# A third kind of expert step, for up to 64 rows, in a block-attention and top-1 expert kernel

## The chip, the core and the metric

The kernel runs on one core of a Trainium2 chip. The metric is device time in microseconds (us) of one execution. Of the core's engines, PE (TensorE) multiplies matrices and its weight loads are listed apart as PEld, DVE (VectorE) and ACT (ScalarE) do elementwise work, POOL (GpSimd) issues the transfers that gather and scatter by index, and SP (SyncE) issues the other transfers. All of SP's transfers go through one queue.

## What is computed

Block-causal attention over 8 batches, 8 heads, 576 positions, head size 64; its output, seen as 4608 rows of 512 numbers, goes through a layer of eight experts of which each row uses one:

```python
e_idx = np.argmax(x @ w_gate, axis=1)
...
for e in range(E):
    mask = e_idx == e
    h = np.maximum(x[mask] @ w1[e], 0.0)      # 512 -> 1024
    ye = h @ w2[e]                            # 1024 -> 512
    out[mask] = gate_w[mask, None] * eom[mask, e, None] * ye
```

All numbers are float32. The kernel splits each float32 operand into a float16 part ("hi") and a bfloat16 rest ("lo"), and multiplies hi by hi, hi by lo and lo by hi, so every product of two tiles is three matmuls. With the inputs drawn, the experts get 896, 0, 1030, 58, 512, 192, 384 and 1536 rows.

## The kernel before

The first half of the span is attention; its matmuls are woven with the flips (transpositions) of the softmax and with the routing. The last stage runs the experts in **steps**. A step takes rows of one expert, in tiles of 128 rows: kind P (pair) two tiles, up to 256 rows; kind S (single) one tile, up to 128 rows. `ORDER` (line 53) lists the kinds in the order in which steps run, `NKIND` how many steps of a kind may ever be needed. The routing (`route_rest`, line 639) counts on the chip how many steps of each kind each expert needs, and writes three small tables, one entry per step: the first row (`rti`), the expert (`wsel`) and whether the weights have to be loaded (`wneed`). Steps that the list `ORDER` can't hold run in a second block behind an `If` on `more`; with these rows the 17 P and 4 S of `ORDER` are just what is needed.

A step i is made of:

- `fetch_ids`, `fetch_x` (POOL): the rows' numbers, then the rows themselves, gathered from `x_d` into `xg`, three and more steps ahead;
- `turn_x`: ACT casts `xg` to `xr` (hi), DVE subtracts (lo), SP transposes both into `xt` by a DMA, two steps ahead;
- `fetch_w` (SP): w1 and w2 of the expert, 2 MB each, in four quarters each, into `w1f` and `w2f`, of which there is one each. An expert that the step before had already is not loaded again (the four issues stand in the queue, but their condition is false); a step of kind S, and a P behind an S, always loads;
- `split_w1`, `split_w2`: ACT casts each quarter to `w1b`/`w2b` (line 777), DVE subtracts (line 778); eight of each per step, loaded anew or not. `w1b` and `w2b` are double, and steps alternate;
- `stage_h` (line 889 PE, 897 ACT, 898 DVE): h = relu(x w1), transposed: 96 matmuls with a 128x128 block of w1 as the stationary operand and the rows as the moving one (256 columns for P, 128 for S), in two halves of 48; after each half ACT takes the relu into `hh` and DVE the rest into `hl`;
- `stage_y` (line 916): per tile of 128 rows 24 matmuls with 128x128 blocks of `hh` or `hl` stationary and w2 moving, 512 columns; ACT scales the result into `ys` (line 919), POOL scatters it to `out` (line 920).

`run` (line 1033) sets the order of the expert stage. In turn i PE does h(i), then y(i-1). ACT and DVE do: relu of the first half of h(i), `turn_x` of step i+2, the split of w1 for step i+1, relu of the second half, the scaling of y(i-1), the split of w2 for step i+1. SP issues w1 and w2 of step i+1 (each quarter when the split before has freed its buffer), then the transposition of step i+2. An engine runs its list strictly in this order.

Of the kernel before, what the change touches and what calls it, by code (L numbers as in the profile page):

```python
# [20 lines left out]
P = 128  # L21
# [5 lines left out]
def block_attention_top1_moe(  # L27
# [22 lines left out]
    SCALE = D ** -0.5  # L50


    ORDER = "PPPPPSPPPPSPPPPSPPPPS"
    KINDS = "PS"
    NKIND = (22, 8)
    FKIND = tuple(ORDER.count(kind) for kind in KINDS)
    BKIND = (0, NKIND[0])
    NSTEP = sum(NKIND)
    NPAIR = NKIND[0]
    NXG = 3  # L60
# [554 lines left out]
        nc.vector.tensor_scalar(row0, t64[:, 0:8:2], fe, None, ALU.add)  # L615


    def sequence(order, i0, used):
        seq = []
        for i, kind in enumerate(order):  # L620
            k = KINDS.index(kind)
            seq.append((BKIND[k] + used[k], 2 - k, i0 + i))
            used[k] += 1
        return seq

    used = [0, 0]
# [12 lines left out]
    def route_rest():  # L639

        cnt = counts(B, "cnt1")
        room, used = sb.tile([P, 2 * NK[4]], F32, name="pt4"), [0]

        def scratch(shape):
            n = 1
            for x in shape:
                n *= x
            used[0] += n
            r = room[:, used[0] - n:used[0]]
            return r.rearrange("p (a b) -> p a b", b=shape[1]) if len(shape) == 2 else r  # L650


        nc.vector.scalar_tensor_tensor(cnt, first, 7 * 64.0 + 1, cnt, ALU.mult, ALU.max)
        big = scratch([E, NTE])
        nc.vector.tensor_tensor(big, bc(cnt, [P, E, NTE], 2), bc(t64, [P, E, NTE], 1), ALU.is_gt)
        nk = small.tile([P, 2, E], F32, name="nk", bufs=1)
        nc.vector.tensor_reduce(nk[:, 0], big[:, :, 2:NTE:4], AX.X, ALU.add)
        nc.vector.tensor_reduce(nk[:, 1], big[:, :, 0:NTE:4], AX.X, ALU.add)
        nc.vector.tensor_tensor(nk[:, 1], nk[:, 1], nk[:, 0], ALU.subtract)

        room3 = sb.tile([P, 2 * NK[3]], F32, name="pt3")[:, 0:3 * E * E].rearrange("p (k a b) -> p k a b", k=3, a=E)
        c1, cm = room3[:, 0], room3[:, 1:3]
        nc.vector.tensor_tensor(c1, upto, bc(first, [P, E, E], 1), ALU.max)
        nc.vector.tensor_tensor(cm, bc(c1, [P, 2, E, E], 1), bc(nk, [P, 2, E, E], 2), ALU.mult)
        cum = small.tile([P, 2, E], F32, name="cum", bufs=1)
        nc.vector.tensor_reduce(cum, cm, AX.X, ALU.add)

        own = small.tile([P, 2, E], F32, name="own", bufs=1)
        nc.vector.tensor_tensor(own, nk, cum, ALU.subtract)
        nc.vector.tensor_tensor(own, own, bc(first, [P, 2, E], 1), ALU.mult)  # L670
        nc.vector.tensor_tensor(cum, cum, own, ALU.add)
        beg = small.tile([P, 2, E], F32, name="beg", bufs=1)
        nc.vector.tensor_tensor(beg, cum, nk, ALU.subtract)
        tot = small.tile([P, 2], F32, name="tot", bufs=1)
        nc.vector.tensor_reduce(tot, cum, AX.X, ALU.max)

        mo = small.tile([P, 1], F32, name="mo", bufs=1)
        nc.vector.tensor_scalar(mo, tot[:, 0:1], float(FKIND[1] - FKIND[0]), tot[:, 1:2], ALU.add, ALU.max)
        nc.vector.tensor_copy(more, mo)

        sh = [P, NSTEP, E]
        inn = scratch(sh[1:])
        ge = scratch(sh[1:])
        parts = [(slice(b, b + n), n) for b, n in zip(BKIND, NKIND)]
        for kind, (sl, n) in enumerate(parts):
            idx = bc(tcol[:, 0:n], [P, n, E], 2)
            nc.vector.tensor_tensor(inn[:, sl], idx, bc(beg[:, kind], [P, n, E], 1), ALU.is_ge)
            nc.vector.tensor_tensor(ge[:, sl], idx, bc(cum[:, kind], [P, n, E], 1), ALU.is_ge)
        nc.vector.tensor_tensor(inn, inn, ge, ALU.subtract)

        nc.vector.tensor_tensor(ge, inn, bc(ecol, sh, 1), ALU.mult)
        et = small.tile([P, NSTEP], F32, name="et", bufs=1)
        nc.vector.tensor_reduce(et, ge, AX.X, ALU.add)
        nc.vector.tensor_copy(wsel, et)
        diff = small.tile([P, NSTEP], F32, name="diff", bufs=1)
        nc.vector.tensor_tensor(diff[:, 1:], et[:, 1:], et[:, 0:NSTEP - 1], ALU.not_equal)
        nc.vector.memset(diff[:, NPAIR:], 1.0)
        for c in fresh:
# [7 lines left out]
        nc.vector.scalar_tensor_tensor(base[:, 1], nk[:, 0], 2.0 * P, e0, ALU.mult, ALU.add)  # L706
        for kind, (sl, n) in enumerate(parts):
# [37 lines left out]
    def fetch_x(st, halves=None):  # L745
        c, n, i = st
        for h in range(*(halves or (0, n))):
            nx = NTOK - 2 * S if 2 * i + h < 3 else NTOK
            nc.gpsimd.indirect_dma_start(
                out=xg[i % NXG][:, h], out_offset=None, in_=x_d[0:nx, :],  # L750
                in_offset=IOA(ap=ids[i][:, h, 0:1].bitcast(U32), axis=0), bounds_check=nx - 1, oob_is_err=False,
            )

    def rows_of(w, ev, j):
# [150 lines left out]
    def stage_y(st, halves=None):  # L905
# [2 lines left out]
        hh, hl = hs[i]  # L908
        w2h, w2l = w2b[b][:, 0], w2b[b][:, 1].bitcast(BF16)
        prods = ((hh, w2h), (hh, w2l), (hl, w2h))  # L910
        for h in range(*(halves or (0, n))):
            py = ps_t.tile([P, 512], F32, name="ps_t")
            k = 0
            for f in range(KF):
                for hv, wv in prods:
                    nc.tensor.matmul(py, hv[:, f, h], wv[:, f, :], start=(k == 0), stop=(k == 3 * KF - 1))  # L916
                    k += 1
            ys = fs.tile([P, DM], F32, name="ys", bufs=4)
            act = nc.scalar.activation(ys, py, AF.Copy, scale=ids[i][:, h, 1:2].bitcast(F32))  # L919
            nc.gpsimd.indirect_dma_start(  # L920
                out=out, out_offset=IOA(ap=ids[i][:, h, 0:1].bitcast(U32), axis=0), in_=ys, in_offset=None,
                bounds_check=NTOK - 1, oob_is_err=False,
            )
# [191 lines left out]
```

## Time and profile before

| | |
|---|---|
| median of three runs (all) | 823.86 us (822.45, 823.86, 830.36) |
| the profiled execution | 826.82 us |
| its span, first to last instruction | 825.1 us |
| PE busy | 764.0 us (93%) |
| DVE, ACT busy | 547.1, 517.5 us |
| clock granted to TensorE, mean | 0.982 of full speed |

A row of the timeline gives a start in us from the beginning of the span, a duration, the engine, the line of the code, the tiles and shapes, and how often the instruction comes in a row; in square brackets the idle time of the engine ahead of it and what ended it. The start of one matmul to the start of the next is what a matmul costs in a stream; its own duration is longer, since they overlap.

### The profile page before, as it was taken

The numbers are of one execution on the slowest core, as the hardware profiler recorded it, in microseconds if no ns is written. First come the engines' busy times: TensorE is split into PE (matmuls) and PEld (weight loads), VectorE is DVE, ScalarE is ACT, GpSimd is POOL, SyncE is SP. The second block draws the span as 40 slices with busy tenths as digits, with TensorE's granted clock in tenths as the row PEclk, the third lists the DMA queues.
The fourth block names the chain that finished last, engine by engine and source line by source line (L and its number), as shares of the span: only waits on it lengthen the run. The fifth ranks groups of instructions, "written<-read, shape, count | busy, mean of one in ns | idle before, by whom it ended". The sixth has DMA issues, their size and how long they took to land. (4 is left out here: it accounts for less than half of the span.)

```text
span 825.1 us, 17693 instructions
## 1 busy us (share of the span) xinstructions
PE 764.0 (93%) x6466; PEld 512.7 (62%) x6466; DVE 547.1 (66%) x1200; ACT 517.5 (63%) x1207; POOL 252.6 (31%) x219
## 2 busy tenths in 40 slices
PE   4899988898989889778999999999999999999994
PEld 3566656565656656555686666676657666676652
DVE  5787858677676767858572866786566656786530
ACT  5788776777758667567513855765556555775530
POOL 4322312424122242447245432233212333200001
PEclk9999999999999999889999999999999999999998
DMA  8998997989898797996029899793789958721601
GB/s 153 168 185 174 192 176 148 176 150 184 173 205 151 155 183 157 191 226 177 28 83 270 152 369 257 220 275 99 249 264 280 274 188 281 179 50 48 230 27 41
DMA packets 255887, 148.25 MB, mean 180 GB/s; under 512 B 224561, under 2 KB 224625, under 8 KB 255793
## 3 DMA queue, kind: packets, MB, share of 16 engines
q1 hardware_dynamic: 247520, 127.76, 69.4%
q0 software_dynamic: 8272, 19.29, 7.6%
q8 instruction: 53, 0.87, 0.5%
q14 instruction: 42, 0.34, 0.1%
HBM read 122.23 MB, written 19.73 MB: 172 GB/s over the span
## 5 line engine op out<-in xcount | busy, mean ns | idle before, releaser
L889 PEld LDWEIGHTS <-w1b 128*128 128x128 f16 (+1 forms) x2112 | 182.6, 98 | 25.2 <-ACT ys L919 2.0
L355 ACT ACTIVATE pt<-ps_s,nbs 128x448 f32<-128x448 f32 (+1 forms) x314 | 164.4, 535 | 41.8 <-DVE nbs L343 17.9
L889 PE MATMUL ps_s<-xt,w1b 128*128 128x256 f16 (+3 forms) x1824 | 182.1, 261 | 1.8 <-DMA xt<-xr 1.5
L916 PE MATMUL ps_t<-w2b,hh 128*128 128x512 f16 x608 | 181.0, 379 | 0.0
L778 DVE TENSOR_TENSOR w2b<-w2f,w2b 128x1024 bf16<-128x1024 f32 x76 | 88.0, 1219 | 113.4 <-ACT w2b L777 113.4
L423 PE MATMUL ps_t<-ident,pt 128*128 128x128 f32 x800 | 124.5, 283 | 8.2 <-DVE xn L472 3.9
L429 ACT COPY pT<-ps_t 128x512 f32<-128x512 f32 (+3 forms) x222 | 96.5, 463 | 56.4 <-PE ps_t L423 55.6
L97 POOL TENSOR_TENSOR sp<-nat,sp 128x1152 f16<-128x1152 f32 x30 | 71.2, 2374 | 152.8 <-DVE nbs L343 91.7
L916 PE MATMUL ps_t<-w2b,hl 128*128 128x512 f16 x304 | 115.2, 379 | 0.0
L919 ACT ACTIVATE ys<-ps_t,ids 128x512 f32<-128x512 f32 x38 | 26.1, 687 | 136.1 <-PE ps_t L916 112.1
L335 PE MATMUL ps_s<-tr,tr 128*128 128x448 f16 (+1 forms) x378 | 98.8, 284 | 11.4 <-ACT pt L355 10.9
L920 POOL DMA_INDIRECT out_dram<-ys,ids x38 | 44.9, 1181 | 185.0 <-ACT ys L919 130.2
L916 PEld LDWEIGHTS <-hh 128*128 128x128 f16 x608 | 59.3, 98 | 66.8 <-issue 0.2
L423 PEld LDWEIGHTS ps_t<-ident,pt 128*128 128x128 f32 x800 | 87.3, 143 | 15.6 <-DVE xn L472 4.2
L336 PE MATMUL ps_s<-sw,tr 128*128 128x448 f16 (+1 forms) x378 | 91.4, 283 | 1.8 <-DMA sw<-tr 1.3
L438 PE MATMUL ps_a<-pT,va 128*64 128x512 f32 (+3 forms) x256 | 85.5, 457 | 6.8 <-DMA va<-in_v_dram 5.7
L778 DVE TENSOR_TENSOR w1b<-w1f,w1b 128x1024 bf16<-128x1024 f32 x76 | 88.1, 1218 | 0.5 <-ACT w1b L777 0.2
L393 DVE TENSOR_REDUCE nmx<-ps_s 128x2 f32<-128x896 f32 (+1 forms) x63 | 60.2, 955 | 41.7 <-PE ps_s L338 41.1
L438 PE MATMUL ps_a<-pT,vb 128*64 128x512 f32 (+3 forms) x256 | 85.6, 458 | 2.0 <-DMA vb<-in_v_dram 2.0
L777 ACT CAST w1b<-w1f 128x1024 f16<-128x1024 f32 x76 | 74.1, 1045 | 1.2 <-DMA w1f<-in_moe_w_dram 1.2
L777 ACT CAST w2b<-w2f 128x1024 f16<-128x1024 f32 x76 | 73.6, 1042 | 0.0
L355 ACT ACTIVATION_READ_ACCUMULATOR pt<-ps_s,nbs 128x1 f32 x314 | 65.2, 208 | 0.0
(203 smaller groups left out, 1080.2 us busy)
## 6 DMA issues: line engine op xcount, KB each, us to landing
w1f<-in_moe_w_dram SPq DMA_DIRECT2D x76, 512.0 KB
w2f<-in_moe_w_dram SPq DMA_DIRECT2D x76, 512.0 KB
nat<-in_k_dram SPq DMA_DIRECT2D x15, 576.0 KB
nat<-in_q_dram SPq DMA_DIRECT2D x15, 576.0 KB
sw<-tr SPq DMA_DIRECT2D x30, 288.0 KB
x_d<-xn SPq DMA_DIRECT2D x32, 256.0 KB
va<-in_v_dram SPq DMA_DIRECT2D x32, 128.0 KB
vb<-in_v_dram SPq DMA_DIRECT2D x64, 64.0 KB
```

What stands on the lines that cost most here:

```text
L97: last_lo[0] = lo.tensor_tensor(sp[:, :, 1, :], self.nats[i], sp[:, :, 0, :], ALU.subtract)
L335: nc.tensor.matmul(ps_ap, qq, k1[ab][:, c0:c1], start=True, stop=False)
L336: nc.tensor.matmul(ps_ap, qq, k2[ab][:, c0:c1], start=False, stop=last)
L355: last_exp[0] = nc.scalar.activation(to, ap, AF.Exp, bias=nbs[0:r, t, ab:ab + 1], scale=SCALE, accum_out=sums[0:r, t, hA + ab:hA + ab + 1],)
L393: nc.vector.tensor_reduce(nmx[:, t, :], pX[:, :, 0:n], AX.X, ALU.max, negate=True)
L423: nc.tensor.transpose(ps[:, i], probs[t][:, col:col + P], ident)
L429: copies[next(nth)](pT[:, r:r + m, Q0[t]:Q0[t] + rows], ps[:, i:i + m, 0:rows])
L438: nc.tensor.matmul(pa[64 * a:64 * a + 64, P * j:512], (va, vb)[a][:, j, :], pT[:, 1 + 2 * j + a, 64 + P * j:576], start=(j == 0), stop=False,)
L777: nc.scalar.copy(hi, src)
L778: eng.tensor_tensor(lo, src, hi, ALU.subtract)
L889: nc.tensor.matmul(ph[:, f4].rearrange("p (h n) -> p h n", n=P), wv[:, cc, f, :], xv[:, cc], start=(k == 0), stop=(k == 3 * KD - 1))
L916: nc.tensor.matmul(py, hv[:, f, h], wv[:, f, :], start=(k == 0), stop=(k == 3 * KF - 1))
```

## The change

A third kind of step, H, takes up to 64 rows. `ORDER` becomes 16 P, 3 S and 3 H, 22 steps where there were 21; the routing counts three kinds. Rows of an expert beyond its full pairs go to an H (1 to 64 rows), an S (65 to 128), an S and an H (129 to 192) or a further P (193 and more). With the rows above:

| | steps in order (kind and expert; * marks those whose weights are loaded) |
|---|---|
| before | P2 P2 P2* P2 P0* S2* P0* P0 P4* P4 S0* P5* P6* P7* P7 S3* P7* P7 P7 P7 S6* |
| after | P2 P2 P2* P2 H2* P0* P0 S0* P0* P4* H3* P4* P6* S5* P7* P7 H5* P7* P7 P7 P7 S6* |

(The first two steps load ahead of the table. Steps count from 0, so H stands at 4, 10 and 16.) H, like S, always loads, and so does a P behind it.

In an H step h has 64 moving columns instead of 128. The second layer is turned (`turned_y`): 96 matmuls with 128x128 blocks of w2 stationary and `hh`/`hl` moving, 64 columns, so the result stands transposed in PSUM; ACT copies it to SBUF, and four transpositions on PE turn it back. These and the scaling and scattering are owed (`owed`, `pay`) until the first quarter of the first half of the next h has been issued. An H step gathers and scatters 64 rows instead of 128.

```diff
-    ORDER = "PPPPPSPPPPSPPPPSPPPPS"
-    KINDS = "PS"
-    NKIND = (22, 8)
+    ORDER = "PPPPHPPSPPHPPSPPHPPPPS"
+    KINDS = "PSH"
+    KTILES = (2, 1, 1)
+    KROWS = (2 * P, P, 64)
+    NKIND = (19, 8, 8)
...
-        nk = small.tile([P, 2, E], F32, name="nk", bufs=1)
-        nc.vector.tensor_reduce(nk[:, 0], big[:, :, 2:NTE:4], AX.X, ALU.add)
-        nc.vector.tensor_reduce(nk[:, 1], big[:, :, 0:NTE:4], AX.X, ALU.add)
-        nc.vector.tensor_tensor(nk[:, 1], nk[:, 1], nk[:, 0], ALU.subtract)
...
+        nc.vector.tensor_reduce(over, big.rearrange("p e (n j) -> p j e n", j=4), AX.X, ALU.add)
+        nk = small.tile([P, NKD, E], F32, name="nk", bufs=1)
+        nc.vector.tensor_copy(nk[:, 0], over[:, 3])
+        nc.vector.tensor_tensor(nk[:, 1], over[:, 1], over[:, 3], ALU.subtract)
+        nc.vector.tensor_tensor(nk[:, 2], over[:, 0], over[:, 2], ALU.add)
+        nc.vector.tensor_tensor(nk[:, 2], nk[:, 2], over[:, 1], ALU.subtract)
+        nc.vector.tensor_tensor(nk[:, 2], nk[:, 2], over[:, 3], ALU.subtract)
...
     def stage_h(*args, **kw):
         for act in h_steps(*args, **kw):
-            pass
+            pay()
         return act
+
+    def pay():
+        while owed:
+            owed.pop()()
...
-        m = h1 - h0
-        xh, xl = (x[:, :, h0:h1] for x in xs[i])
+        m, w = h1 - h0, width[i]
+        xh, xl = (x[:, :, h0:h1, 0:w] for x in xs[i])
...
+        if width[i] < P:
+            return turned_y(st, prods)
...
+    def turned_y(st, prods):
+
+        i = st[2]
+        w = width[i]
+        pt = ps_a.tile([P, 512], F32, name="ps_a")[:, 0:KD * w].rearrange("p (c n) -> p c n", c=KD)
+        for c in range(KD):
+            k = 0
+            for f in range(KF):
+                for hv, wv in prods:
+                    nc.tensor.matmul(
+                        pt[:, c], wv[:, f, P * c:P * c + P], hv[:, f, 0, 0:w], start=(k == 0), stop=(k == 3 * KF - 1)
+                    )
+                    k += 1
+        yt = fs.tile([P, DM], F32, name="ys", bufs=4)[:, 0:KD * w].rearrange("p (c n) -> p c n", c=KD)
+        act = nc.scalar.copy(yt, pt)
+
+        def rest():
+            py = ps_t.tile([P, 512], F32, name="ps_t")
+            for c in range(KD):
+                nc.tensor.transpose(py[0:w, P * c:P * c + P], yt[:, c], ident)
+            put(i, 0, py)
+
+        owed.append(rest)
+        return act
...
         stage_y(seq[n - 1])
+        pay()
```

(`put` is the scaling and scattering that stood in `stage_y`, for `w` rows; the other lines of the routing only widen a table from two kinds to three.)

ACT around the second layer of a single step, before: in turn 16, the scaling of y(15), a step S, stands between the relu of h(16)'s second half and the split of w2 for step 17 (line 777 is the cast, 897 the relu, 919 the scaling).

```order
L897 ACTIVATE hh<-ps_s 128x1024
L919 ACTIVATE ys<-ps_t,ids 128x512
L777 CAST w2b_6600<-w2f_6595 128x1024
L777 CAST w2b_6600<-w2f_6596 128x1024
L777 CAST w2b_6600<-w2f_6597 128x1024
L777 CAST w2b_6600<-w2f_6598 128x1024
L897 ACTIVATE hh<-ps_s 128x1024
```

The same place around the second layer of the first H step, y(4), after the change: turn 5 (line 790 is now the cast, 914 the relu, 943 the scaling, 964 the new copy).

```order
L914 ACTIVATE hh<-ps_s 128x1024
L964 COPY ys<-ps_a 128x256
L790 CAST w2b_6610<-w2f_6605 128x1024
L790 CAST w2b_6610<-w2f_6606 128x1024
L790 CAST w2b_6610<-w2f_6607 128x1024
L790 CAST w2b_6610<-w2f_6608 128x1024
L943 ACTIVATE ys<-ps_t,ids 64x512
L914 ACTIVATE hh<-ps_s 128x1024
```

The copy takes the place of the scaling, and the scaling, of 64 partitions, has moved behind the four casts of w2 and ahead of the relu of the next h, h(6).

PE in the first half of h(6), after the change, where the first quarter of it ends (line 906 is the first layer, 969 the transposition back).

```order
L906 MATMUL ps_s<-xt,w1b_6609 128x256
L906 LDWEIGHTS w1b_6609
L906 MATMUL ps_s<-xt,w1b_6609 128x256
L969 MATMUL ps_t<-ident,ys 64x128 x4
L906 LDWEIGHTS w1b_6609
L906 MATMUL ps_s<-xt,w1b_6609 128x256
```

The four transpositions of step 4 stand behind 12 matmuls of h(6), which don't need them; before, nothing stood between the quarters of an h.

## Rows read from the trace of the kernel before

**Rows 1.** The page: the span, and busy time, share of the span and instructions of each engine.

```profile
span 825.1 us, 17693 instructions
PE 764.0 (93%) x6466; PEld 512.7 (62%) x6466; DVE 547.1 (66%) x1200; ACT 517.5 (63%) x1207; POOL 252.6 (31%) x219
```

**Rows 2.** Busy times by stretch: the middle of the expert stage, and the tail behind the last matmul. Columns: stretch and its length, busy time and count of instructions of PE, PEld, DVE, ACT and POOL, the granted clock, the DMA engines' busy share, GB/s.

```profile
574.00:689.00 115.00, 115.00 (x845) 78.40 (x843) 74.12 (x72) 69.03 (x83) 31.07 (x28) 1.00 0.83 248
...
816.00:825.10 9.10, 0.00 (x0) 0.00 (x0) 0.00 (x0) 0.00 (x0) 0.98 (x1) 0.65 0.08 31
```

**Rows 3.** The same view of three turns: h(8) and y(7), both of kind P; h(10) of kind S and y(9) of kind P; h(11) of kind P and y(10) of kind S.

```profile
563.80:584.65 20.85, 20.85 (x146) 14.11 (x145) 12.09 (x11) 11.41 (x13) 4.57 (x4) 1.00 0.49 152
605.48:621.20 15.72, 15.72 (x146) 10.06 (x144) 11.57 (x12) 10.95 (x14) 3.60 (x3) 1.00 0.86 233
621.20:636.86 15.66, 15.66 (x122) 11.74 (x120) 12.70 (x12) 11.21 (x13) 2.94 (x3) 1.00 1.05 315
```

**Rows 4.** Timeline of PE at three places of the attention stage with narrow matmuls in a row, each with its own 128x128 weights.

```profile
92.82 0.24 PE L539 MATMUL ps_t<-oh,ones 128*128 128x32 f16 x4
92.92 0.18 PE L542 MATMUL ps_t<-run_cnt,ones 128*128 128x40 f16 x1
...
212.64 0.19 PE L335 MATMUL ps_s<-tr,tr 128*128 128x64 f16 x1
212.67 0.19 PE L336 MATMUL ps_s<-sw,tr 128*128 128x64 f16 x1
212.70 0.19 PE L338 MATMUL ps_s<-mneg,mrow 128*128 128x64 bf16 x1
212.73 0.42 PE L423 MATMUL ps_t<-ident,pt 128*128 128x128 f32 x2
...
214.93 0.19 PE L336 MATMUL ps_s<-sw,tr 128*128 128x64 f16 x1
214.96 0.19 PE L335 MATMUL ps_s<-tr,tr 128*128 128x64 f16 x1
214.99 0.19 PE L336 MATMUL ps_s<-sw,tr 128*128 128x64 f16 x1
215.01 0.25 PE L335 MATMUL ps_s<-tr,tr 128*128 128x192 f16 x1
```

**Rows 5.** Timeline of PE at the beginning and behind the end of h(5), of kind S, 96 matmuls of 128 columns.

```profile
511.58 0.61 PE L889 MATMUL ps_s<-xt,w1b 128*128 128x128 f16 x8
...
516.94 0.59 PE L916 MATMUL ps_t<-w2b,hh 128*128 128x512 f16 x2
```

**Rows 6.** Groups of instructions by form: the weight loads of h, and DVE's rest of h in the shapes of P and S.

```profile
L889 PEld LDWEIGHTS <-w1b 128*128 128x128 f16 x1408 | 129.9, 98 | 17.8 <-ACT ys L919 2.0
L898 DVE SCALAR_TENSOR_TENSOR hl<-ps_s,hh 128x1024 bf16<-128x1024 f32 x32 | 39.0, 1219 | 1.7 <-ACT hh L897 1.7
L898 DVE SCALAR_TENSOR_TENSOR hl<-ps_s,hh 128x512 bf16<-128x512 f32 x12 | 8.1, 686 | 7.2 <-ACT hh L897 7.2
```

**Rows 7.** Timeline of PE: four 128x128 float32 transpositions in the middle of y's matmuls, and the only long wait of PE in the expert stage.

```profile
440.79 0.60 PE L840 MATMUL ps_a<-ident,xg 128*128 128x128 f32 x4
441.23 0.59 PE L916 MATMUL ps_t<-w2b,hh 128*128 128x512 f16 x2
...
458.65 0.60 PE L889 MATMUL ps_s<-xt,w1b 128*128 128x256 f16 x4 [1.54 <-DMA xt<-xr]
```

**Rows 8.** Timeline of ACT, then DVE, around h(7) (its `turn_x` has two tiles of rows).

```profile
543.21 0.69 ACT L919 ACTIVATE ys<-ps_t,ids 128x512 f32<-128x512 f32 x1 [3.72 <-issue]
...
548.40 1.02 ACT L897 ACTIVATE hh<-ps_s 128x1024 f16<-128x1024 f32 x1 [0.73 <-PE ps_s L889]
...
544.86 4.63 DVE L778 TENSOR_TENSOR w2b<-w2f,w2b 128x1024 bf16<-128x1024 f32 x4 [2.97 <-ACT w2b L777]
549.46 1.22 DVE L898 SCALAR_TENSOR_TENSOR hl<-ps_s,hh 128x1024 bf16<-128x1024 f32 x1
550.60 1.28 DVE L855 TENSOR_TENSOR xr<-xg,xr 128x512 bf16<-128x512 f32 x2
551.80 4.62 DVE L778 TENSOR_TENSOR w1b<-w1f,w1b 128x1024 bf16<-128x1024 f32 x4
```

**Rows 9.** Timeline of SP around the loads of steps 12 and 13 (a transposition is held until the transfers ahead of it in the queue have moved), and the busy times of the two stretches between the ends of those transpositions.

```profile
613.88 4.18 SPq L861 DMA_TRANSPOSE xt<-xr  x1
619.66 2.94 SPq L770 DMA_DIRECT2D w1f<-in_moe_w_dram  x4
624.35 3.78 SPq L770 DMA_DIRECT2D w2f<-in_moe_w_dram  x4
630.19 5.61 SPq L861 DMA_TRANSPOSE xt<-xr  x1
...
645.85 7.90 SPq L861 DMA_TRANSPOSE xt<-xr  x1
...
617.90:635.50 17.60, 17.60 (x131) 12.62 (x129) 13.46 (x14) 11.21 (x13) 4.49 (x4) 1.00 1.10 298
635.50:653.40 17.90, 17.90 (x133) 12.74 (x131) 12.99 (x13) 11.89 (x14) 5.06 (x5) 1.00 1.11 324
```

**Rows 10.** The routing: busy times of its stretch, and the timeline of POOL where it first reads what the routing has written.

```profile
418.20:428.30 10.10, 10.09 (x80) 7.47 (x79) 9.72 (x44) 2.52 (x3) 5.33 (x5) 1.00 0.14 44
...
432.66 2.32 POOL L738 DMA_DIRECT2D ids<-tab_d  x3
```

More of the change, by code (lines that the diff above doesn't have):

```diff
@@ L50, in block_attention_top1_moe @@
     SCALE = D ** -0.5
-    ORDER = "PPPPPSPPPPSPPPPSPPPPS"
-    KINDS = "PS"
-    NKIND = (22, 8)
+    ORDER = "PPPPHPPSPPHPPSPPHPPPPS"
[3 more added lines that the diff above has]
+    NKIND = (19, 8, 8)
     FKIND = tuple(ORDER.count(kind) for kind in KINDS)
-    BKIND = (0, NKIND[0])
+    BKIND = tuple(sum(NKIND[:j]) for j in range(len(NKIND)))
     NSTEP = sum(NKIND)
@@ L615, in route_first @@
         nc.vector.tensor_scalar(row0, t64[:, 0:8:2], fe, None, ALU.add)
+    width = {}
     def sequence(order, i0, used):
@@ L621, in sequence @@
             k = KINDS.index(kind)
-            seq.append((BKIND[k] + used[k], 2 - k, i0 + i))
+            seq.append((BKIND[k] + used[k], KTILES[k], i0 + i))
+            width[i0 + i] = KROWS[k] // KTILES[k]
             used[k] += 1
         return seq
-    used = [0, 0]
+    used = [0] * len(KINDS)
     steps = sequence(ORDER, 0, used)
@@ L655, in route_rest @@
         nc.vector.tensor_tensor(big, bc(cnt, [P, E, NTE], 2), bc(t64, [P, E, NTE], 1), ALU.is_gt)
-        nk = small.tile([P, 2, E], F32, name="nk", bufs=1)
-        nc.vector.tensor_reduce(nk[:, 0], big[:, :, 2:NTE:4], AX.X, ALU.add)
-        nc.vector.tensor_reduce(nk[:, 1], big[:, :, 0:NTE:4], AX.X, ALU.add)
-        nc.vector.tensor_tensor(nk[:, 1], nk[:, 1], nk[:, 0], ALU.subtract)
-        room3 = sb.tile([P, 2 * NK[3]], F32, name="pt3")[:, 0:3 * E * E].rearrange("p (k a b) -> p k a b", k=3, a=E)
@@ L662, in route_rest @@
-        c1, cm = room3[:, 0], room3[:, 1:3]
+        NKD = len(KINDS)
+        pt3 = sb.tile([P, 2 * NK[3]], F32, name="pt3")
+        over = pt3[:, (NKD + 1) * E * E:(NKD + 1) * E * E + 4 * E].rearrange("p (j e) -> p j e", e=E)
+        nc.vector.tensor_reduce(over, big.rearrange("p e (n j) -> p j e n", j=4), AX.X, ALU.add)
+        nk = small.tile([P, NKD, E], F32, name="nk", bufs=1)
+        nc.vector.tensor_copy(nk[:, 0], over[:, 3])
+        nc.vector.tensor_tensor(nk[:, 1], over[:, 1], over[:, 3], ALU.subtract)
@@ L663, in route_rest @@
+        nc.vector.tensor_tensor(nk[:, 2], over[:, 0], over[:, 2], ALU.add)
+        nc.vector.tensor_tensor(nk[:, 2], nk[:, 2], over[:, 1], ALU.subtract)
+        nc.vector.tensor_tensor(nk[:, 2], nk[:, 2], over[:, 3], ALU.subtract)
+        room3 = pt3[:, 0:(NKD + 1) * E * E].rearrange("p (k a b) -> p k a b", k=NKD + 1, a=E)
+        c1, cm = room3[:, 0], room3[:, 1:NKD + 1]
         nc.vector.tensor_tensor(c1, upto, bc(first, [P, E, E], 1), ALU.max)
-        nc.vector.tensor_tensor(cm, bc(c1, [P, 2, E, E], 1), bc(nk, [P, 2, E, E], 2), ALU.mult)
@@ L665, in route_rest @@
-        cum = small.tile([P, 2, E], F32, name="cum", bufs=1)
+        nc.vector.tensor_tensor(cm, bc(c1, [P, NKD, E, E], 1), bc(nk, [P, NKD, E, E], 2), ALU.mult)
+        cum = small.tile([P, NKD, E], F32, name="cum", bufs=1)
         nc.vector.tensor_reduce(cum, cm, AX.X, ALU.add)
-        own = small.tile([P, 2, E], F32, name="own", bufs=1)
+        own = small.tile([P, NKD, E], F32, name="own", bufs=1)
         nc.vector.tensor_tensor(own, nk, cum, ALU.subtract)
-        nc.vector.tensor_tensor(own, own, bc(first, [P, 2, E], 1), ALU.mult)
+        nc.vector.tensor_tensor(own, own, bc(first, [P, NKD, E], 1), ALU.mult)
@@ L671, in route_rest @@
         nc.vector.tensor_tensor(cum, cum, own, ALU.add)
-        beg = small.tile([P, 2, E], F32, name="beg", bufs=1)
+        beg = small.tile([P, NKD, E], F32, name="beg", bufs=1)
         nc.vector.tensor_tensor(beg, cum, nk, ALU.subtract)
-        tot = small.tile([P, 2], F32, name="tot", bufs=1)
+        tot = small.tile([P, NKD], F32, name="tot", bufs=1)
         nc.vector.tensor_reduce(tot, cum, AX.X, ALU.max)
@@ L678, in route_rest @@
         nc.vector.tensor_scalar(mo, tot[:, 0:1], float(FKIND[1] - FKIND[0]), tot[:, 1:2], ALU.add, ALU.max)
+        nc.vector.scalar_tensor_tensor(mo, tot[:, 2:3], float(FKIND[1] - FKIND[2]), mo, ALU.add, ALU.max)
         nc.vector.tensor_copy(more, mo)
@@ L700, in route_rest @@
         nc.vector.tensor_copy(wneed, diff)
-        base = small.tile([P, 2, E], F32, name="base", bufs=1)
+        base = small.tile([P, NKD, E], F32, name="base", bufs=1)
         e0 = small.tile([P, E], F32, name="e0", bufs=1)
@@ L706, in route_rest @@
         nc.vector.scalar_tensor_tensor(base[:, 1], nk[:, 0], 2.0 * P, e0, ALU.mult, ALU.add)
+        nc.vector.scalar_tensor_tensor(base[:, 2], nk[:, 1], 1.0 * P, base[:, 1], ALU.mult, ALU.add)
         for kind, (sl, n) in enumerate(parts):
@@ L749, in fetch_x @@
             nc.gpsimd.indirect_dma_start(
-                out=xg[i % NXG][:, h], out_offset=None, in_=x_d[0:nx, :],
-                in_offset=IOA(ap=ids[i][:, h, 0:1].bitcast(U32), axis=0), bounds_check=nx - 1, oob_is_err=False,
+                out=xg[i % NXG][0:width[i], h], out_offset=None, in_=x_d[0:nx, :],
+                in_offset=IOA(ap=ids[i][0:width[i], h, 0:1].bitcast(U32), axis=0), bounds_check=nx - 1, oob_is_err=False,
             )
@@ L879, in h_steps @@
         h0, h1 = halves or (0, n)
-        m = h1 - h0
-        xh, xl = (x[:, :, h0:h1] for x in xs[i])
+        m, w = h1 - h0, width[i]
+        xh, xl = (x[:, :, h0:h1, 0:w] for x in xs[i])
         for half in range(2):
-            ph = ps_s.tile([P, 4, m * P], F32, name="ps_s", padded_shape=[P, 4, 256])
+            ph = ps_s.tile([P, 4, m * w], F32, name="ps_s", padded_shape=[P, 4, 256])
             for f4 in range(4):
@@ L889, in h_steps @@
                         nc.tensor.matmul(
-                            ph[:, f4].rearrange("p (h n) -> p h n", n=P), wv[:, cc, f, :], xv[:, cc], start=(k == 0), stop=(k == 3 * KD - 1)
+                            ph[:, f4].rearrange("p (h n) -> p h n", n=w), wv[:, cc, f, :], xv[:, cc], start=(k == 0), stop=(k == 3 * KD - 1)
                         )
@@ L895, in h_steps @@
             fsl = slice(4 * half, 4 * half + 4)
-            pv = ph.rearrange("p f (h n) -> p f h n", n=P)
-            act = nc.scalar.activation(hh[:, fsl, h0:h1], pv, AF.Relu)
+            pv = ph.rearrange("p f (h n) -> p f h n", n=w)
+            act = nc.scalar.activation(hh[:, fsl, h0:h1, 0:w], pv, AF.Relu)
             nc.vector.scalar_tensor_tensor(
-                hl[:, fsl, h0:h1], pv, 0.0, hh[:, fsl, h0:h1], ALU.max, ALU.subtract
+                hl[:, fsl, h0:h1, 0:w], pv, 0.0, hh[:, fsl, h0:h1, 0:w], ALU.max, ALU.subtract
             )
@@ L917, in stage_y, with put @@
                     k += 1
[L918 to L923, printed above, removed]
-        return act
-    ids, xs, hs = {}, {}, {}
+            act = put(i, h, py)
+        return act
+    def put(i, h, py):
+        w = width[i]
+        ys = fs.tile([P, DM], F32, name="ys", bufs=4)
+        act = nc.scalar.activation(ys[0:w], py[0:w], AF.Copy, scale=ids[i][0:w, h, 1:2].bitcast(F32))
+        nc.gpsimd.indirect_dma_start(
+            out=out, out_offset=IOA(ap=ids[i][0:w, h, 0:1].bitcast(U32), axis=0), in_=ys[0:w], in_offset=None,
+            bounds_check=NTOK - 1, oob_is_err=False,
+        )
+        return act
+    def turned_y(st, prods):
+        i = st[2]
+        w = width[i]
+        pt = ps_a.tile([P, 512], F32, name="ps_a")[:, 0:KD * w].rearrange("p (c n) -> p c n", c=KD)
[5 more added lines that the diff above has]
+                        pt[:, c], wv[:, f, P * c:P * c + P], hv[:, f, 0, 0:w], start=(k == 0), stop=(k == 3 * KF - 1)
+                    )
+                    k += 1
[7 more added lines that the diff above has]
+        owed.append(rest)
+        return act
+    ids, xs, hs, owed = {}, {}, {}, []
     loads = {2 * u - (4 if u == len(units) - 1 else 3): load_heads(u) for u in range(2, len(units))}
```

## The prediction

> **What bounds the kernel now.** I read the page first: a span of 825.1 us with PE busy for 764.0 [rows 1]. Then the busy times by stretch: in the middle of the expert stage PE is busy for 115.00 of 115.00 us at full granted clock, DVE for 74.12 and ACT for 69.03 [rows 2]. The expert stage is bound by what PE streams; its one long wait is 1.54 us ahead of h(2) [rows 7]. Behind the last matmul lie some 9 us of scattering that the change doesn't touch [rows 2]. So a step costs its matmuls, and the question is whether what feeds them (splits on ACT and DVE, weights through SP's queue) still hides beneath a shorter PE list.
>
> **What a P and an S cost.** A turn of two P halves (h and y) takes 20.85 us, and columns divide it evenly: h streams 96 x 256 columns, y 48 x 512, so 10.4 us each. Turns with one S part take 15.72 (its h) and 15.66 (its y) [rows 3]; an S costs 15.72 + 15.66 - 20.85 = 10.53. The change takes out one P and one S: **-31.4 us**.
>
> **What an H costs.** It has 96 + 96 matmuls of 64 columns, each with new 128x128 weights, and four transpositions. Narrow matmuls stand in the attention stage only a few in a row: 64 columns follow each other after 0.09 / 3 = 0.030 and 0.08 / 3 = 0.027 us, and matmuls of 32 columns and fewer after 0.10 / 4 = 0.025, with a weight load ahead of each [rows 4]. Long runs exist at 128 columns: 96 in 516.94 - 511.58 = 5.36 us, 0.056 each [rows 5]. No row shows 96 of 64 columns. Bounds: below, 0.025, the floor of the narrowest; above, 0.098, the duration of a weight load by itself [rows 6], as if none were hidden. I take 0.0285, between the two 64-column rows: they are the same shape, and a load beneath a matmul is hidden in each of them. h and y then cost 96 x 0.0285 = 2.74 us each. Four float32 transpositions take 441.23 - 440.79 = 0.44 [rows 7]. ACT's copy, which they wait for, has a quarter of the next h (2.6 us) as cover. An H: 2 x 2.74 + 0.44 = 5.9; three: **+17.8 us**. PE's list gets shorter by 31.4 - 17.8 = 13.6.
>
> [...]
>
> **Splits beside a shorter PE list.** Each step still casts and subtracts all its weights on ACT and DVE, so an H asks for nearly as much there as an S: 11.57 us of DVE in an S turn [rows 3]. Two places get tight.
> First, h(i) of a P followed by y(i-1) of an H. From the middle of h(i) PE has 5.2 + 2.7 = 7.9 us until it needs w1 of step i+1. DVE's part behind that middle runs from its rest of h (549.46) to the end of the split (551.80 + 4.62 = 556.42), 6.96 us, or 6.3 when the step two ahead has one tile of rows; it starts 1.06 after the relu (548.40) [rows 8], and the relu as the half ends. That is 7.4 at steps 5 and 11 (an S is two ahead) and 8.0 at step 17: hidden twice, and 0.1 too late there.
> Second, h of the H itself. DVE is done with the split of w2 6.3 us after the scaling starts (543.21 to 544.86 + 4.63) [rows 8], which it does as PE ends the y before. Then come the rest of h (686 ns at 512 columns, 1219 at 1024 [rows 6], so some 0.4 at 256), two subtractions (1.28) and the split of w1 (4.62): 12.6. PE has 2.7 + 10.4 = 13.1. It fits by 0.5.
> I take **+0.5** in all, for the time from one engine to the next at six tight places; from 0 to 3 x 1 us if DVE comes a little later at each place.
>
> **Weights through SP's queue.** Loaded steps rise from 12 to 14, and 7 to 14 become eight in a row (before, 10 to 13 were the longest run). Where loads follow each other, the queue is full: the transposition behind a load is held until w2 has landed, and the ends of three such holds, 618.06, 635.80 and 653.75, lie 17.7 and 18.0 us apart, with DMA share 1.10 and 1.11 [rows 9]. So a loaded step takes 17.85 us of queue. PE needs w1 of steps 8 to 14 at intervals from middle of h to middle of h (half h, the y between, half h): 18.2, 18.2, 15.6, 17.0, 17.0, 13.5, 18.2, in all 117.7, where the queue wants 7 x 17.85 = 125. Behind by, added up: -0.4, -0.7, 1.5, 2.4, 3.2, 7.6, 7.2. Two cushions. Step 6 loads nothing, so w1 of step 7 is asked for right behind that step's own transposition: after the middle of h(5) 2.9 on DVE (1.06 + 1.22 + 0.6), some 1 to transpose, 1.6 on SP (618.06 to 619.66) and 7.0 for 2.1 MB at 298 GB/s [rows 8, 9], 12.5 against a need at 5.2 + 2.7 + 0.4 + 5.2 = 13.5: 1.0 early. And PE can wait for the split until h itself starts: a slack of 5.2 + 2.7 - 7.4 = 0.5 at step 12 (behind the y of an H), 5.2 + 10.4 - 8.0 = 7.6 at step 13, and 2.6 + 10.4 - 8.0 = 5.0 at 14. So step 12 waits 3.2 - 1.0 - 0.5 = 1.7, which moves the later needs by as much, and steps 13 and 14 are covered (7.6 and 7.2 less 1.0, 1.7 and their slack). The H at step 10 halves one transposition on the way, so I take **+1.0**. Bounds: 0; and, if every hold were the longest row, 7.90 instead of 5.61, 2.3 more per step, five intervals to step 12: +11.
>
> **Routing.** Eight more small DVE instructions join 44 that take 9.72 us [rows 10], about 1 us by their size. POOL reads the table first at 432.66 [rows 10], over 4 us behind, and PE's wait ahead of h(2) would swallow 1.5 us of lateness: nothing; without these covers, 1 us. Copies, widths and gathers of 64 rows: nothing on PE.
>
> **The sum.** -31.4 + 17.8 + 0.5 + 1.0 = -12.1. The profiled execution took 826.8, so 814.7; it lies 3.0 above the median of the runs, 823.9, which I predict from: **811.8 us**, 1.5% faster. About 1%, 8.2 us, is what a measurement here can tell from no change: 815.6 and 832.1 are the bounds.
>
> **Rivals.**
> *Weight loads come through (slower).* In a run of 96 nothing but loads and short matmuls is there to hide them. At 0.098 each [rows 6] an H costs 19.3 and the change is -31.4 + 57.8 = +26: 850 us. It turns to a loss from (31.4 / 3 - 0.44) / 192 = 0.052 on. For it: no long run at 64 columns; against it: every short one in rows 4. [...]
> *The stream keeps the pace of 128 columns.* At 0.056 [rows 5] an H is 11.2, the change +2: 826. Against it: 0.025 to 0.030 in rows 4.
> *The queue becomes the bound.* If the cushions aren't there, the 7.2 us by which the eight loads fall behind come back, less the 1.0 in the sum: -12.1 + 6.2 = -5.9: 818. For it: DMA share above 1 in rows 9; against it: the cushions above, which leave 1 to 2 us.
> *The change doesn't do what it says:* the kinds needed (16, 3, 3) are those of the list, so the block behind the `If` stays out; no chance worth a number.
>
> **Chances.** Forecast 0.68 (its own range 808.5 to 815: 576 narrow matmuls at 0.027 or 0.030 make 1 us either way, the waits 0 to 3, the median of the runs another 1 to 2); queue 0.17 (815.6 to 822); pace of 128 columns 0.08 (824 to 828); weight loads 0.07 (above 832). So faster 0.68, same 0.17 + 0.08 = 0.25, slower 0.07. The range leaves out the last two cases and a little: 807 to 822.
>
> **What would show it.** Right: matmuls of lines 906 and 959 in an H step start 0.028 to 0.030 apart, three times; PE's list shorter by 13 to 14 us between h(3) and the end; idle time ahead of h(5), h(12) and h(18) under 1 us each. Wrong: starts 0.05 or more apart; waits for w1 on DVE or DMA ahead of h(12) to h(14) of several us; a granted clock below 1.00 behind such a wait.

## The result, and the profile after

The kernel after the change takes 798.3 us at the median (797.11 to 801.09, four runs), the kernel before 823.9: a ratio of 0.9705, 95% interval 0.967 to 0.974, 25.5 us faster where the prediction said 12.1. The direction was right; the gain is twice the sum.

The profiled executions (826.8 and 798.7 us) show where it is. I cut both spans at the same two matmuls: the last one that counts rows for the routing (line 588, now 590), and the last one of all. Timeline of PE of the kernel before at these two places:

```profile
417.21 0.18 PE L588 MATMUL ps_t<-run_cnt,ones 128*128 128x8 f16 x1 [0.42 <-DVE run_cnt L547]
...
813.96 0.38 PE L916 MATMUL ps_t<-w2b,hl 128*128 128x512 f16 x1
```

And of the kernel after:

```profile
403.20 0.18 PE L590 MATMUL ps_t<-run_cnt,ones 128*128 128x8 f16 x1 [0.41 <-DVE run_cnt L549]
...
785.98 0.38 PE L935 MATMUL ps_t<-w2b,hl 128*128 128x512 f16 x1
```

From the counts to the end, which is the part that the change edits, it went from 396.75 to 382.78 us: 14.0 less, where the sum had 12.1. But the counts themselves come 14.0 us earlier. Up to there, on every engine, both kernels run the same instructions in the same order (some neighbouring matmuls of `va` and `vb` change places in the records, as they do between two executions of one kernel). The prediction has no term for that stretch.

The page of after, which answers to [rows 1]: PE is busy for 17.8 us less, in a span that is 28.0 shorter.

```profile
span 797.1 us, 18412 instructions
PE 746.2 (94%) x6768; PEld 508.3 (64%) x6790; DVE 557.0 (70%) x1220; ACT 525.0 (66%) x1220; POOL 261.2 (33%) x220
```

**The expert stage.** Timeline of PE at the first H step: h(4), y(4), and the four transpositions with the next row behind them (they answer to [rows 4, 5] and [rows 7]).

```profile
475.63 2.96 PE L906 MATMUL ps_s<-xt,w1b 128*128 128x64 f16 x96
478.43 0.38 PE L935 MATMUL ps_t<-w2b,hh 128*128 128x512 f16 x1
...
499.27 0.22 PE L959 MATMUL ps_a<-hh,w2b 128*128 128x64 f16 x2
...
502.07 1.48 PE L906 MATMUL ps_s<-xt,w1b 128*128 128x256 f16 x12
503.38 0.60 PE L969 MATMUL ps_t<-ident,ys 128*64 128x128 f32 x4
503.82 2.35 PE L906 MATMUL ps_s<-xt,w1b 128*128 128x256 f16 x20
```

Start to start, h(4) takes 478.43 - 475.63 = 2.80 us, y(4) 502.07 - 499.27 = 2.80 and the transpositions 0.44: 96 matmuls at 0.029 each, 6.0 for an H, where the prediction had 5.9; h(10) and h(16), y(10) and y(16) take 2.80 each as well. The longest waits of PE from the counts to the end (columns: total us, times, longest):

```profile
PE ps_s L906 <- DVE hl L915: 0.6, 1, 0.6
PE ps_s L906 <- DVE w1b L791: 0.5, 2, 0.3
PE ps_t L590 <- DVE run_cnt L549: 0.4, 1, 0.4
```

PE itself never waits for a DMA there; the 1.54 us ahead of h(2) in [rows 7] is gone. Yet the queue is as full as in [rows 9]. Timeline of SP where eight loads follow each other:

```profile
583.71 4.81 SPq L874 DMA_TRANSPOSE xt<-xr  x1
...
597.12 6.76 SPq L874 DMA_TRANSPOSE xt<-xr  x1
...
613.13 8.59 SPq L874 DMA_TRANSPOSE xt<-xr  x1
...
632.08 7.17 SPq L874 DMA_TRANSPOSE xt<-xr  x1
```

The holds end at 588.52, 603.88, 621.72 and 639.25, 15.4, 17.8 and 17.5 apart, with one of 8.59 us. The cushions cover most of it: in h(12) PE waits 0.2 us, not 1.7. Timeline of ACT, then of PE, in h(12):

```profile
601.23 1.05 ACT L790 CAST w1b<-w1f 128x1024 f16<-128x1024 f32 x1 [2.34 <-DMA w1f<-in_moe_w_dram]
...
603.59 0.28 PE L906 MATMUL ps_s<-xt,w1b 128*128 128x256 f16 x1 [0.21 <-DVE w1b L791]
```

So what stands behind PE's wait for the split is the queue, at the step that the prediction named: the cast of the last quarter waits 2.34 us for its load.

The stretch from h(4), the first H step, to the last matmul has the H steps alone, without the routing. Busy times, first of before (where h(4) is a P), then of after (columns as in [rows 2]):

```profile
490.74:813.97 323.23, 323.23 (x2401) 218.59 (x2399) 202.61 (x193) 189.97 (x225) 74.87 (x64) 1.00 0.67 194
```

```profile
475.63:785.98 310.35, 309.29 (x2709) 214.82 (x2723) 210.53 (x203) 197.29 (x238) 80.51 (x67) 1.00 0.75 231
```

That is 12.9 us less.

**The attention stage.** The same instructions, but not the same transfers. Busy times from 20 to 395 us, first of before, then of after (columns as in [rows 2]; the last three are granted clock, DMA share, GB/s):

```profile
20.00:395.00 375.00, 337.06 (x3168) 221.62 (x3168) 274.43 (x840) 271.17 (x888) 127.72 (x93) 0.97 0.92 175
```

```profile
20.00:395.00 375.00, 346.81 (x3301) 229.26 (x3300) 280.54 (x861) 279.00 (x904) 132.09 (x98) 0.98 0.83 176
```

After, as many GB/s move with the DMA engines busy for 0.83 of the time in place of 0.92. The instruction of SP's queue that changed most is the transposition of q and k (`turn`, line 102, now 104). All of its 30 instructions on SP's queue, by their tile `tr` (columns: shortest, median and longest in ns, first and last start), before and after:

```profile
L102 SPq DMA_TRANSPOSE tr<-sp x30: 2484/2820/4735, 15.1 to 345.9; - x30
```

```profile
L104 SPq DMA_TRANSPOSE tr<-sp x30: 1753/2072/3953, 13.8 to 330.4; - x30
```

2.82 us at the median became 2.07, some 22 us of one queue over 30 of them.

**What the change did to them.** The tables `rti`, `wsel` and `wneed` have one entry per possible step, 30 before and 35 after. They stand in SBUF ahead of everything that is allocated later, and in the two compiled programs each of them grows from 128 to 160 bytes per partition. So the tiles of the pools `sb`, `ld` and `fb` that attention's transfers and the experts' loads use lie elsewhere: before, each begins 160 bytes behind a multiple of 256, after, each begins at one. And what the transposition reads is rows of `sp` of 64 hi and 64 lo float16 numbers: 256 bytes. The loads of q and k write rows of 256 bytes too, 64 float32 numbers of `nat`, which lies in `ld` with `sp`.

### The profile page after: what moved, and what is told of

The parts are those of the page before. It is cut to its first block, busy times and chain, and to the rows that moved or that the text cites. A ratio compares the mean times of both kernels' runs of the same rounds, so it can differ in the third digit from the quotient of the medians.

```text
span 797.1 us, 18412 instructions
## 1 busy us (share of the span) xinstructions
PE 746.2 (94%) x6768; PEld 508.3 (64%) x6790; DVE 557.0 (70%) x1220; ACT 525.0 (66%) x1220; POOL 261.2 (33%) x220
## 5 line engine op out<-in xcount | busy, mean ns | idle before, releaser
L906 PEld LDWEIGHTS <-w1b 128*128 128x128 f16 (+1 forms) x2208 | 176.4, 98 | 22.1 <-DVE w1b L791 1.8
L906 PE MATMUL ps_s<-xt,w1b 128*128 128x256 f16 (+5 forms) x1920 | 175.4, 253 | 0.5 <-DVE w1b L791 0.5
L935 PE MATMUL ps_t<-w2b,hh 128*128 128x512 f16 (+1 forms) x538 | 162.1, 379 | 0.0
L791 DVE TENSOR_TENSOR w2b<-w2f,w2b 128x1024 bf16<-128x1024 f32 x80 | 92.7, 1221 | 89.3 <-ACT w2b L790 89.3
L935 PE MATMUL ps_t<-w2b,hl 128*128 128x512 f16 x280 | 106.1, 379 | 1.2
L944 POOL DMA_INDIRECT out_dram<-ys,ids x38 | 55.1, 1450 | 157.6 <-ACT ys L943 76.4
L943 ACT ACTIVATE ys<-ps_t,ids 128x512 f32<-128x512 f32 (+1 forms) x38 | 26.1, 686 | 109.5 <-PE ps_t L935 90.9
L935 PEld LDWEIGHTS <-hh 128*128 128x128 f16 x560 | 54.4, 98 | 62.3 <-issue 1.2
L791 DVE TENSOR_TENSOR w1b<-w1f,w1b 128x1024 bf16<-128x1024 f32 x80 | 92.6, 1220 | 2.1 <-ACT w1b L790 2.1
L790 ACT CAST w1b<-w1f 128x1024 f16<-128x1024 f32 x80 | 78.2, 1045 | 3.3 <-DMA w1f<-in_moe_w_dram 3.2
```

The costliest lines, as they stand in the source:

```text
L790: nc.scalar.copy(hi, src)
L791: eng.tensor_tensor(lo, src, hi, ALU.subtract)
L906: nc.tensor.matmul(ph[:, f4].rearrange("p (h n) -> p h n", n=w), wv[:, cc, f, :], xv[:, cc], start=(k == 0), stop=(k == 3 * KD - 1))
```

## The experiments

My theory: reading 256 bytes takes the DMA engines longer where the read crosses a multiple of 256, and the change, by the size of its tables, moved `sp` onto one. The rivals: something in the change's instructions; a multiple of 64 or 128 is enough; it is the writing side (`tr`, `va`); any transfer gains. The runs below come from three chips (below, the later chips), on which the kernel before takes longer: 836.8 us at the median beside the first four kernels, 838.6 beside the next four, 837.1 beside the last four. So I compare ratios, and absolute times only between kernels that ran side by side.

### Unused bytes, and nothing else

In the first three, only the size of `wneed` changes (56, 40 and 48 entries), no instruction:

```diff
-    wneed = const.tile([P, NSTEP], I32, name="wneed")
+    wneed = const.tile([P, NSTEP], I32, name="wneed", padded_shape=[P, 56])
```

> The kernel before, with 96 unused bytes per partition behind the table wneed, as much as the three tables rti, wsel and wneed grow by in the change (35 entries in place of 30, each table rounded up to 32 bytes). No instruction is added or moved. The tiles that attention and the loads of the experts use (tr0, tr1, sw, va, vb, nat, sp, w1f, w2f, xr, xt) then begin at a multiple of 256 bytes, as they do after the change, where before they begin 160 behind one. Theory of the addresses (the attention stage got faster because its transfers' 256-byte packets meet better addresses): the 14 us that came ahead of the counts of the routing come back without the change, 823.9 - 14 = 810, within 807 to 813. Rival (it is something in the change's own instructions, or in its order): 823.9, within 822 to 826.

> The kernel before, with 32 unused bytes per partition behind wneed: the same tiles begin 192 bytes behind a multiple of 256, which is a multiple of 64, as after the change. If a multiple of 64 is enough: 810, as with 96 bytes. If it has to be a multiple of 256: 824, no change. Rival (not the addresses): 824 too.

> The kernel before, with 64 unused bytes per partition behind wneed: the same tiles begin 224 bytes behind a multiple of 256, and 32 behind one of 64, as before. Theory of the addresses, by 64 or by 256: 824, no change. [...]

The fourth is the kernel after with 80 entries there:

> The kernel after the change, with 160 unused bytes per partition behind wneed: the tiles begin 160 bytes behind a multiple of 256 again, as in the kernel before. Theory of the addresses: the attention stage falls back by some 14 us and what is left is the change of the expert steps: 798.3 + 14 = 812, within 809 to 815 (the sum of the prediction was 811.8). Rival: 798.3, within 797 to 801.

| | `nat`, `sp` and `tr` begin behind a multiple of 256 by | ratio to before, 95% interval | transposition, median |
|---|---|---|---|
| 96 bytes in before | 0 | 0.9885 (0.983 to 0.994) | 2.02 us |
| 32 bytes in before | 192 | 1.0007 (0.998 to 1.004) | 2.80 us |
| 64 bytes in before | 224 | 1.0032 (1.000 to 1.007) | 2.79 us |
| 160 bytes in after | 160 | 0.9852 (0.978 to 0.993) | 2.79 us |

The transpositions of before with 96 bytes, beside those of after above:

```profile
L102 SPq DMA_TRANSPOSE tr<-sp x30: 1752/2019/3997, 14.9 to 342.5; - x30
```

96 bytes that nobody uses make the kernel before 1.15% faster (some 10 us, 5 to 14 by the interval; I had expected 14); 32 and 64 bytes bring no gain. So a multiple of 64 is not enough, and a shift as such does nothing. Taking the good addresses away from the kernel after leaves 0.9852 of 836.8, 12.4 us. The prediction had forecast 12.1 for the whole change; with an interval of 6 to 19 us it is chance that the two lie so close. The two parts multiply to 0.974.

### Reading or writing, 256 or 128

Bytes behind a small table between the pools move `ld` (`nat`, `sp`) alone; 96 for the first and 224 for the third. For the second, 96 bytes behind `wneed` and 160 here move all but `ld`.

```diff
-        tot = small.tile([P, 2], F32, name="tot", bufs=1)
+        tot = small.tile([P, 2], F32, name="tot", bufs=1, padded_shape=[P, 32])
```

> The kernel before, with 96 unused bytes behind the small table tot, which lies between the pools sb and ld: only nat and sp, the tiles of pool ld, begin at a multiple of 256; tr0, tr1, sw, va, vb and the tiles of the expert stage stay 160 behind one. sp is what the transpositions of attention read. Theory that the packets' reading side decides: as with both pools moved, 0.9885 of before. Theory that the writing side decides: 1.00. If each has a part: 0.994.

> The kernel before, with 96 unused bytes behind wneed and 160 behind tot: tr0, tr1, sw, va, vb and in the expert stage w1f, w2f, xr and xt begin at a multiple of 256; nat and sp stay 160 behind one. Reading side (of sp) decides: 1.00 of before, but for what v's loads and the expert stage give. Writing side decides: 0.9885. Each has a part: 0.994.

> The kernel before, with 224 unused bytes behind tot: only nat and sp move, to 128 bytes behind a multiple of 256. Theory that a packet of 256 bytes is read well only from a multiple of 256: 1.00 of before, transpositions of attention as slow as there (2.8 us at the median on SP's queue). If a multiple of 128 is enough: 0.988, as with 96 bytes, and 2.0 us.

The same row, of the kernel with `ld` alone at a multiple of 256:

```profile
L102 SPq DMA_TRANSPOSE tr<-sp x30: 1755/2056/4044, 14.8 to 345.5; - x30
```

With everything but `ld` there:

```profile
L102 SPq DMA_TRANSPOSE tr<-sp x30: 2417/2776/5007, 14.9 to 353.7; - x30
```

With `ld` at 128 behind one:

```profile
L102 SPq DMA_TRANSPOSE tr<-sp x30: 2439/2770/4871, 15.1 to 352.8; - x30
```

The ratios are 0.9882 (0.984 to 0.993), 0.9968 (0.994 to 1.000) and 0.9971 (0.994 to 1.000). `ld` alone brings all of the gain; all other tiles bring 0.6% at most, by the interval, and no more than the third kernel, which has nothing at a multiple of 256. And 128 is not enough. The granted clock isn't the cause: with `ld` alone moved the profiled execution took 830.9 us at a mean clock of 0.978, and two executions of the kernel before beside it 837.0 and 839.1 at 0.977.

This settles it for 256, but not for the reading side: `ld` holds `sp`, which is read, and `nat`, which is written, and these runs move both. The trace shows that both gain. From 2 to 13.5 us SP's queue has six loads into `nat` and no transposition yet. Busy times there, first with everything but `ld` at a multiple of 256, then with `ld` alone:

```profile
2.00:13.50 11.50, 5.36 (x52) 4.36 (x53) 6.33 (x16) 3.79 (x7) 5.32 (x13) 1.00 1.21 205
```

```profile
2.00:13.50 11.50, 5.21 (x52) 4.44 (x53) 7.44 (x16) 3.99 (x7) 5.35 (x12) 1.00 0.90 205
```

The same 205 GB/s take a DMA share of 1.21 or 0.90, where only the side that is written differs. So my theory had one side too few. How much of the 1.2% comes from `nat` and how much from `sp` no run here shows.

One place where the queue's time reaches the engines is DVE's waits for `x_d<-xn`, a store that stands in SP's queue among the transpositions. All waits of this kind up to the counts, with 64 bytes in before (no gain), then with 96 (columns: total us, times, longest):

```profile
DVE xn L472 <- DMA x_d<-xn: 10.0, 7, 2.7
```

```profile
DVE xn L472 <- DMA x_d<-xn: 4.1, 5, 2.5
```

It is 9.7 to 10.2 us in the kernels before whose `ld` lies badly (8.2 in after with 160 bytes), and 3.2 to 4.1 in every one whose `ld` lies well, some 6 us less. How much of these 6 reaches PE, and where the rest of the 10 us comes from, is not shown.

### The same kernel again, and the second layer not turned

> The kernel after the change as it is, again, beside the kernel before and the three kernels below on one chip. Both theories of the attention stage and the result of the first runs: 0.970 of the kernel before, within 0.965 to 0.976, as the two parts 0.9885 and 0.9852 multiply to 0.974.

It was 816.83 us, 0.9733 (0.967 to 0.980). And the turned layer taken out, so that an H's second layer is like that of an S:

```diff
-        if width[i] < P:
-            return turned_y(st, prods)
...
-                    nc.tensor.matmul(py, hv[:, f, h], wv[:, f, :], start=(k == 0), stop=(k == 3 * KF - 1))
+                    nc.tensor.matmul(py[0:width[i]], hv[:, f, h, 0:width[i]], wv[:, f, :], start=(k == 0), stop=(k == 3 * KF - 1))
```

> The kernel after the change with the second layer of H not turned: per H 24 matmuls of 512 columns with 128x64 blocks of hh and hl stationary, as a step S has, in place of 96 of 64 columns and four transpositions. By the prices of the prediction 3 x (5.21 - 2.74 - 0.44) = +6.1 us against the kernel after, 1.0076 of it. Rival (that a turned layer is worth nothing, since ACT, DVE or the queue bound a short step): 1.000. If 64 stationary columns make a matmul of 512 columns cheaper: between.

It was 823.85 us, 0.9832 (0.979 to 0.988): 7.0 more than the kernel after beside it, where 6.1 was expected. Busy times from h(4) to the last matmul, first with the layer not turned, then of the kernel after on the same chip:

```profile
492.32:809.02 316.70, 315.77 (x2481) 212.69 (x2495) 210.66 (x203) 196.38 (x235) 76.11 (x66) 1.00 0.77 225
```

```profile
493.92:804.01 310.09, 309.24 (x2709) 215.03 (x2723) 211.01 (x203) 197.60 (x238) 77.28 (x66) 1.00 0.76 228
```

So the turned layer is worth 6.6 us there, 6.5 of it PE's busy time, and no new wait takes any of it back. From the counts to the end the two executions differ by 389.77 - 385.59 = 4.2 only, since the kernel after has waits of PE ahead of its first H step that the other lacks:

```profile
457.53 0.60 PE L935 MATMUL ps_t<-w2b,hh 128*128 128x512 f16 x2 [0.54 <-ACT hh L914]
...
462.00 0.50 PE L906 MATMUL ps_s<-xt,w1b 128*128 128x256 f16 x3 [0.53 <-DVE w1b L791]
463.13 1.05 PE L906 MATMUL ps_s<-xt,w1b 128*128 128x256 f16 x8 [0.63 <-DVE w1b L791]
...
493.92 2.96 PE L906 MATMUL ps_s<-xt,w1b 128*128 128x64 f16 x96
```

They are not the turned layer's: they come before it first runs, and the kernel `right` below, which turns its layer as well, has none of them.

### Narrower still, and the other side of SBUF

The pace of the narrow matmuls, with half of an H step's rows:

```diff
-    KROWS = (2 * P, P, 64)
+    KROWS = (2 * P, P, 32)
```

> The kernel after the change with 32 rows per H step in place of 64: rows 32 to 63 of each H step are left out. Its time is of no interest, the pace of h(4) and y(4) is: they took 2.80 us each for 96 matmuls of 64 columns, 0.029 each. [...] If something that every matmul with its own weights has sets it: 0.029 still, 2.8 us.

Timeline of PE at h(4) and the matmul behind it:

```profile
497.54 2.56 PE L906 MATMUL ps_s<-xt,w1b 128*128 128x32 f16 x96
499.94 0.59 PE L935 MATMUL ps_t<-w2b,hh 128*128 128x512 f16 x2
```

499.94 - 497.54 = 2.40, 0.025 each: the pace of the shortest matmuls in [rows 4] holds in a long run, and half the columns do take time off the 0.029 at 64, so that isn't a cost of the weight loads alone.

> The kernel after the change with 224 unused bytes at the end of pool wp: the tiles on the right side (xg0, xg1, hh, hl, xh, xl, ys, w1b0, w2b0), which begin 224 bytes behind a multiple of 256 before and after, begin at one. Theory that it is the reading of short packets of 256 bytes that pays: no change, 1.000 of the kernel after, since only the rows scattered from ys (2048 bytes) are read there, and few packets. If every transfer gains by good addresses: the tail behind the last matmul and the gathers get shorter, 1 to 3 us less.

> The kernel after the change as it is, beside the one above: 0.970 to 0.975 of before.

```diff
+            wp.tile([P, 56], F32, name="gap")
```

814.17 us, 0.9736 (0.969 to 0.978), beside 813.24, 0.9714 (0.966 to 0.977), of the kernel after: no difference. Good addresses for gathers of 2 KB and scatters bring nothing here, and I found no version faster than the kernel after.

## Why the prediction was half right

- **What bounds the kernel.** Right for the expert stage. From h(4) on PE is busy for all but some 1 us of the stretch, which takes 323.2 us in all seven kernels with the instructions of before, and 310.0 to 311.2 in five executions with those of after: 12.0 to 13.2 less, where the sum had 12.1. One of the five is after with 160 bytes (310.4), so addresses do nothing there. The other 1.1 of the 14.0 lie between the counts and h(4), where the wait ahead of h(2) went away.
- **P, S and H.** Right: 6.0 us for an H where 5.9 stood. The rival of weight loads that come through and that of the pace of 128 columns are out: 0.029, not 0.098 or 0.056.
- **Splits and queue.** The sum had 0.5 and 1.0 us. From h(4) on PE waits for `w1b` only in h(12): 0.2 us in after and 0.87 (at 618.15) in `after_third`, nothing above 0.1 in the other three. The place of the queue's term is right and its size at most 0.9; for the splits' 0.5 nothing is seen. The rival of the queue as the bound is out: with holds up to 8.59 us PE waits for the queue, by way of the split, for at most 0.9.
- **Routing: the step that failed.** "Eight more small DVE instructions" were costed, and "Copies, widths and gathers of 64 rows" set to "nothing on PE". The width of the three tables was costed by the instructions that write them. But a table's width also decides where the tiles behind it begin. That is worth -1.15% by itself on one of the later chips (-9.6 us, interval 5 to 14). On the first chip, where it wasn't tested by itself, 11 to 14 us lie ahead of the counts: 25.5 in all less the 14.0 of the expert stage, or the 14.0 between the two profiled executions. The sum went from "-31.4" to "+1.0" without an entry for the stage that the diff doesn't edit, and the range, made from the sum's own terms, could not hold it. Its lower end, 807.0, left 5 us for everything unknown.
- **The routing's own time.** From the counts to h(4) it is 73.0 to 73.5 us in the kernels before, 72.4 and 73.0 in two executions of the five of after and 74.3 to 75.5 in the other three, with waits like those shown above. The sum had nothing here, or 1 us without its covers. Whether these waits are the longer routing's doing stays open.
- **What could have been seen.** [rows 2] give the DMA share of the middle of the expert stage and of the tail; the attention stage, at a share of 0.92, has no row. That share says that a transfer's price may count there. The addresses were to be had from the two compiled programs.

Open: why the attention stage takes longer on the later chips. The expert stage of before takes 396.75 us on the first and 396.24 to 396.55 on the later ones in six kernels with its instructions, so the whole difference between the chips lies ahead of the counts.

## What to carry to other kernels

A change that alters the size of any tile moves all tiles behind it: compare the base addresses of the two programs, and look at those that a transfer reads or writes in short rows, before writing "nothing" for a stage that the diff leaves alone. Put a tile that a DMA reads or writes in rows of 256 bytes at a multiple of 256; a few unused bytes do it, and here 96 of them were worth nearly as much (0.9885 of before) as the new kind of step (0.9852). Give each stage of the profile a line in the sum, with the resource that is busy there, even where its code stays the same.

## What the hardware showed

Where the 256-byte rows that a transfer reads or writes in SBUF begin, behind a multiple of 256, sets their price in these runs. In the trace's records of packets, 9,216 packets of 256 bytes come before the first transposition in every run, all of them of loads into `nat`: one takes 17.9 ns in the mean where `ld` begins at a multiple of 256, and 22.5 to 24.0 where it doesn't. Up to the counts there are 179,712. Given to SP's transfers in the order in which these stand in its queue, they took in the mean:

| `ld` begins behind a multiple of 256 by | 0 | 128 | 160 | 192 | 224 |
|---|---|---|---|---|---|
| loads of q and k, which write `nat`, ns | 18.0 | 20.8 | 21.0 to 21.4 | 21.5 | 21.8 |
| transpositions, which read `sp`, ns | 21.4 to 22.4 | 24.7 | 24.8 to 25.3 | 25.9 | 25.0 |
| all 256-byte packets, ns | 20.1 to 20.9 | 23.2 | 22.9 to 23.6 | 23.9 | 24.5 |

From before to the kernel with `ld` alone moved, the loads go from 98 to 83 us of the 16 engines' time, the transpositions from 109 to 93. (For v's loads, into tiles of `sb`, the runs differ too much to tell.) On the page the same is the queue q1, packets, MB and share of the span of 16 engines, first of before, then of before with 96 bytes:

```profile
q1 hardware_dynamic: 247520, 127.76, 69.4%
```

```profile
q1 hardware_dynamic: 247520, 127.76, 63.4%
```

0.694 x 825.1 = 573 us and 0.634 x 823.6 = 522, for the same packets.

The read of `sp` from a multiple of 256 is the cheap one, 21.4 to 22.4 ns; among the other columns its price doesn't rise with the offset: 24.7 at 128, 25.9 at 192, 25.0 at 224. The loads into `nat` do rise in the order of the columns, from 18.0 to 21.8 ns. Why a row that begins elsewhere costs more, no run here shows.

The other surprise is small: 96 matmuls in a row with new 128x128 weights each follow at 0.029 us for 64 columns and 0.025 for 32, though the profile gives a weight load 98 ns [rows 6].
